# Reordering the first units of a fused state-space scan and two-layer projection on one Trainium2 core

## The chip, the cores and the metric

The kernel runs on one core of a Trainium2 chip. The time is that of the device in microseconds (us); lower is better. The engines are called as the profile calls them: PE (TensorE, with PEld for its weight loads), DVE (VectorE), ACT (ScalarE), POOL (GpSimd) and SP (SyncE, here a queue that issues DMAs).

## The reference

Two blocks follow each other. The first is a gated linear recurrence over the sequence, for 4 batches and 8 heads, 768 steps each, with head width 32 and state width 16. Inputs are x, a decay a for each step, B and C:

```
for chunk c:                     # log_a = log(clip(a, 1e-6, 1)); cum = cumsum of it in the chunk
    M       = (C_c B_c^T) * exp(cum_i - cum_j) * causal
    y_c     = M x_c + (C_c state) * exp(cum_i)
    state   = exp(sum of log_a) * state + sum_j (B_j x_j^T) * exp(cum_end - cum_j)
```

The result y, as 3072 rows of 256, goes through the second block: h = y w_in (256 x 2048), g = h * sigmoid(h), out = g w_out (2048 x 256). The two weight matrices arrive in 64 bits and are cut down to 32 by the kernel itself.

## The kernel before, in words

The sequence is cut into chunks of 64 steps, and 256 steps of one batch form a unit; there are 12 units (u = 0 to 11), three for a batch. Two units form a pair P, whose 512 rows go through the second block at a time. Nothing is scheduled by a compiler: the order of the calls in the source is the order of the instructions in each engine's queue, and a queue runs strictly in that order. Semaphores stand where one engine needs another's result or a buffer.

The recurrence of a unit consists of these steps.

- f_P0 clips a (laid over the partitions, tile pa01 for units 0 and 1, pa2 for unit 2) into pz; it runs on POOL at L337. f_P scans it to running products pfx on DVE (L341). f_C multiplies C with them into cw (L400; for unit 0 on POOL, else on DVE).
- f_Ab (L354 to L358) broadcasts the clipped a from 12 rows (ach) to 128 partitions with a PE matmul by a selection matrix, into one PSUM bank (8 heads of 64 steps). There are two for a unit (k = 0, 1). f_Ek (L360) runs scan_E (L346 to L352) over it on DVE: products of a between all pairs of steps in a chunk, tile E. Units 0 to 1 get it so; later units load the rows by DMA instead (load_ab, f_E1).
- f_B (L370) weights B into BT (DVE). f_TP (L382) transposes B, and for unit 1 and 2 also C, on PE. For the first unit of a batch C is loaded in another layout and transposed on DVE by f_T (L378). f_T2 (L396, ACT) splits C by odd and even heads into ce.
- f_G (L424) is C times B on PE and writes the PSUM tile gy; f_D0 (L408) is BT times x on PE, into other columns of the same tile. f_M (L434, DVE) multiplies G into E, once for each k; f_S (L438, DVE) carries the state over the four chunks; f_SM (L453, ACT) masks the states.
- f_Y (L460) makes y on PE, f_X (L484) copies it out on ACT (tile xf).

The weights come in blocks of 256 columns or rows, n = 0 to 15: load_w loads the raw block (SP's queue), w_size (ACT, L193 and L196) and w_bits (DVE, L201, L203, L204, then one add on POOL, L209, in one or two parts) cut it to 32 bits (tile w). POOL's add is the last step, and PE's projection waits for it.

The pair 0 goes through the second block in plain 32-bit products: f_s1(u, j) (L515) is h for block j and one unit, four matmuls and a Silu on ACT; f_s2(j) (L526) adds block j of the second product. From pair 1 on each 32-bit product is done in three faster parts: w_h, w_l (ACT, with an accumulating DMA on POOL's queue) and w_d (DVE) split the weights, f_xh, f_xl and f_xd split y, and s1_d, s1_h and s2, s2_d (L543 to L604) multiply them. step(s), for s = 0 to 82, runs this for pairs 1 to 5 and puts the recurrence of the next pair in between (PLAN). It fills most of the time: from about 80 us on.

Ahead of step(0) the order is written out by hand, in two parts. L654 to L723 is a list of calls for units 0 and 1, weight blocks 0 to 5 and the loads of units 2 and 3. L782 to L790 is the table `steps`, where each entry (u, j, text) is f_s1(u, j) followed by the steps of the text, and then six texts for f_s2. In a text "2:PTC1" means steps P, T, C and the first half of the scan (f_E1) for unit 2; D is f_G and f_D0, S is f_S, s is f_SM, M is f_M twice, Y is f_Y and f_X, and small h, l, d are the parts of y. A step without a colon is one for the weights: b is w_bits, s w_size, h, l, d the three parts, r the load of a raw block, m f_s2, and p s1_d.

At the start PE has nothing to work on. busy (L289) fills this with matmuls of zeros from tile misc (`idle`), which DVE clears at L283; further fills stand at L659 and L671. SP's queue begins with ach (L237), C of unit 0 (L246), a for units 0 and 1 (L249), x of unit 0 (L250) and three raw weight blocks. ACT's queue issues B of unit 0 and C of unit 1 (L247, L248). POOL's queue issues two small stores of f_A0 (L287) and x of unit 2 (L709).

Of the kernel before, what the change touches and what calls it, by code (L numbers as in the profile page):

```python
# [11 lines left out]
BF16 = mybir.dt.bfloat16  # L12
# [21 lines left out]
def kernel(  # L34
# [22 lines left out]
    nc = tc.nc  # L57

    batch, H, S, D = x.shape
# [30 lines left out]
    def half(name):  # L90
        return ps_h.tile([128, 512], FP32, name=name, tag="h")
# [7 lines left out]
    ab, bn, tbc, xt, PZ = ({} for _ in range(5))  # L99
# [16 lines left out]
    def load_n(u, i, q):  # L116
        b, t0 = at(u)
        if i == 0:
            t = bn[u] = (block("bn0")[:, 0:256].rearrange("p (k h n) -> p k h n", k=2, h=H) if u in (0, 1, 3) else
                         loads.tile([128, 2, H, N], FP32, name="bn"))  # L120
        else:
            t = tbc[u] = block("tbc0")[:, 0:256].rearrange("p (k h n) -> p k h n", k=2, h=H)
        for k in range(2):
            q.dma_start(out=t[:, k], in_=(B, C)[i][b, :, t0 + 128 * k:t0 + 128 * k + 128].rearrange("h p n -> p h n"))
# [18 lines left out]
    def load_x(u, q):  # L143
        b, t0 = at(u)
        xt[u] = loads.tile([128, 2, H, D], FP32, name="xt", bufs=2)
        for k in range(2):
            q.dma_start(out=xt[u][:, k], in_=x[b, :, t0 + 128 * k:t0 + 128 * k + 128].rearrange("h p d -> p h d"))
# [41 lines left out]
    def w_size(n, what="uv"):  # L189
        if n in raw:  # L190
            if "u" in what:
                u = wu[n] = block("wu")
                nc.scalar.activation(two(u), raw[n][:, :, :, 1].bitcast(FP32), AF.Abs)  # L193
            if "v" in what:
                v = wv[n] = block("wv")
                nc.scalar.activation(two(v), raw[n][:, :, :, 0], AF.Copy, scale=2.0 ** -51, bias=2.0)  # L196

    def w_bits(n, parts=1):
        if n in raw:
            u, v, hi = two(wu.pop(n)), two(wv.pop(n)).bitcast(U32), raw[n][:, :, :, 1]  # L200
            nc.vector.tensor_scalar(out=u, in0=u, scalar1=LEAST, scalar2=MOST, op0=ALU.max, op1=ALU.min)  # L201
            u = u.bitcast(U32)
            nc.vector.tensor_scalar(out=u, in0=u, scalar1=3, scalar2=None, op0=ALU.logical_shift_left)  # L203
            nc.vector.scalar_tensor_tensor(out=v, in0=hi, scalar=0x80000000, in1=v,  # L204
                                           op0=ALU.bitwise_and, op1=ALU.bitwise_or)
            w32[n] = block("w32")
            for i in range(parts):
                fs = slice(WF // parts * i, WF // parts * (i + 1))
                nc.gpsimd.tensor_tensor(out=two(w32[n])[:, :, fs].bitcast(U32), in0=u[:, :, fs], in1=v[:, :, fs],  # L209
                                        op=ALU.add)  # L210
        if n == 3:
            load_w(n + RAW, nc.sync)
# [22 lines left out]
    A0, A1 = 96, 96 + NC0  # L235
    ach = block("ach").rearrange("p (h t) -> p h t", t=Q)
# [8 lines left out]

    load_t(0, 1, nc.sync)  # L246
    load_n(0, 0, nc.scalar)  # L247
    load_n(1, 1, nc.scalar)  # L248
    load_a(pa01, 0, 2 * UT)  # L249
    load_x(0, nc.sync)  # L250
    for n in range(3):
        load_w(n, nc.sync)
    load_n(1, 0, nc.sync)
# [31 lines left out]
    def f_A0():  # L285
        for t in (a_in[:, :, 0:1].rearrange("h c t -> c h t"), a_zero[:, :, 0:1]):
            nc.gpsimd.dma_start(out=t, in_=misc[:NC1, 0:H].rearrange("p (h t) -> p h t", t=1))  # L287

    def busy(n, small=0):  # L289
        t = half("zero")  # L290
        for i in range(n):
            nc.tensor.matmul(out=t, lhsT=idle[:, 0:128], rhs=idle, start=True, stop=True)
        for i in range(small):
            nc.tensor.matmul(out=t[:64, :64], lhsT=idle[:, 0:64], rhs=idle[:, 64:128], start=True, stop=True)
# [3 lines left out]
    sel = block("sel").rearrange("p (s c t) -> p s c t", s=4, c=2)  # L298
# [11 lines left out]
        nc.gpsimd.affine_select(out=diag1, in_=diag1, pattern=[[0, 1], [-1, Q]], compare_op=ALU.not_equal,  # L310
                                fill=1.0, base=-64 * c, channel_multiplier=1)
    nc.scalar.activation(misc[:, 2 * UT - 1:], idle[:, 0:1], AF.Silu)
    busy(5)
    f_A()
    hm = const.tile([128, H], FP32, name="hm")
    nc.gpsimd.memset(hm, 1.0)
# [17 lines left out]
    def f_P0(u, engine):  # L334
        src = (pa2[:, 0:UT] if u == 2 else pa01[:, UT * u:UT * u + UT]).rearrange("p (c t) -> p c t", t=Q)
        PZ[u] = (pz, pz1, pz)[u]
        engine.tensor_scalar(out=PZ[u][:, :, 1:], in0=src, scalar1=1.0, scalar2=1e-6, op0=ALU.min, op1=ALU.max)  # L337
# [8 lines left out]
    def scan_E(u, g0, n, t):  # L346
        if g0 == 0:
            E[u] = sc.tile([128, 2, H, Q], FP32, name="E")
        nc.vector.tensor_tensor_scan(out=E[u].rearrange("p k h t -> p (k h t)")[:, Q * g0:Q * (g0 + n)],  # L349
                                     data0=t.rearrange("p g t -> p (g t)"),  # L350
                                     data1=diag[:, 0:n].rearrange("p g t -> p (g t)"),
                                     initial=0.0, op0=ALU.mult, op1=ALU.add)  # L352

    def f_Ab(u, k):  # L354
        ab[u, k] = t = acc("ab").rearrange("p (h t) -> p h t", t=Q)
        nc.tensor.matmul(out=t.rearrange("p h t -> p (h t)"),  # L356
                         lhsT=sel[:A1, 2 * u + k].rearrange("r c m -> r (c m)"),
                         rhs=ach[:A1].rearrange("r h t -> r (h t)"), start=True, stop=True)  # L358

    def f_Ek(u, k):  # L360
        scan_E(u, H * k, H, ab.pop((u, k)))

    def f_E1(u, i, n):
        g = 2 * H // n
# [5 lines left out]
    def f_B(u, ks=slice(0, 2)):  # L370
        if u not in BT:
            BT[u] = sc.tile([128, 2, H, N], FP32, name="BT")
        nc.vector.tensor_tensor(out=BT[u][:, ks], in0=bn[u][:, ks],
                                in1=E[u][:, ks, :, Q - 1:Q].to_broadcast([128, ks.stop - ks.start, H, N]), op=ALU.mult)
# [33 lines left out]
    def f_D0(u, ts=(0, 1, 2, 3)):  # L408
        last = u % UPB == UPB - 1
        bt = BT[u].rearrange("p k h n -> p k (h n)")  # L410
        xc = xt[u].rearrange("p k h d -> p k (h d)")
        d = [new_dp(u)[:, c, 256:384].rearrange("p (k x) -> p k x", k=2) for c in range(2)]
        for t in ts[:3 if last else 4]:
            k, c = divmod(t, 2)
            for g in range(4):
                nc.tensor.matmul(out=d[c][32 * g:32 * g + 32, k],
                                 lhsT=bt[64 * c:64 * c + 64, k, 32 * g:32 * g + 32],
                                 rhs=xc[64 * c:64 * c + 64, k, 64 * g:64 * g + 64], start=True, stop=True,
                                 tile_position=(64 * c, 32 * g), skip_group_check=True)
        BX[u] = d  # L420
        if 3 in ts:
            BT.pop(u)

    def f_G(u):  # L424
        bh, ce, dp = BH.pop(u), CE.pop(u), new_dp(u)
        for k in range(2):
            for c in range(2):
                ts = slice(128 * k + 64 * c, 128 * k + 64 * c + 64)
                for g in range(4):
                    nc.tensor.matmul(out=dp[64 * c:64 * c + 64, g, 128 * k:128 * k + 128],  # L430
                                     lhsT=bh[32 * g:32 * g + 32, ts], rhs=ce[32 * g:32 * g + 32, :, ts],
                                     start=True, stop=True, tile_position=(32 * g, 64 * c), skip_group_check=True)

    def f_M(u, k):  # L434
        m = E[u].rearrange("p k (g e) t -> p k g (e t)", e=2)
        nc.vector.tensor_tensor(out=m[:, k], in0=DP[u][:, :, 128 * k:128 * k + 128], in1=m[:, k], op=ALU.mult)
# [216 lines left out]

    f_P0(0, nc.gpsimd)  # L654
    f_P0(1, nc.gpsimd)
    f_Ab(0, 0)
    f_Ab(0, 1)
    f_TP(0)
    busy(2, 18)  # L659
    f_Ek(0, 0)  # L660
    f_Ek(0, 1)
    f_B(0)
    f_D0(0)
    f_T(0, 1)
    for e in range(2):
        f_T2(0, e)
    w_size(0, "u")
    f_P(0)
    f_C(0, nc.gpsimd)
    f_A0()  # L670
    busy(1, 10)  # L671
    f_G(0)
    f_S(0)
    f_SM(0)
    w_size(0, "v")
    f_M(0, 0)
    f_M(0, 1)
    w_bits(0, 2)
    f_Ab(1, 0)
    w_size(1)  # L680
# [14 lines left out]
    load_n(2, 0, nc.scalar)  # L695
    f_P(1)
    f_C(1)
    f_P0(2, nc.gpsimd)
    w_bits(2, 2)
    f_G(1)  # L700
    f_D0(1)
# [9 lines left out]
    load_w(7, nc.sync)  # L711
    load_w(8, nc.sync)
    w_bits(3, 2)
    f_Y(1)
    f_X(1)
    w_size(4)
# [55 lines left out]
    def todo(text):  # L772

        for step in text.split():
            if ":" in step:
# [3 lines left out]
            n = int(step[1:].split(".")[0])  # L779
            {"b": w_bits, "s": w_size, "h": w_h, "l": w_l, "d": w_d, "m": f_s2, "p": s1_d, "r": load_r}[step[0]](n)  # L780

    steps = ((1, 0, ""), (0, 3, "2:PTC1 s6"), (1, 1, "b5 2:2Ba"), (1, 2, "3:x b6 r11 s7"), (1, 3, "b7 r12 s8"),  # L782
             (0, 4, "2:DSsM r13"), (1, 4, "b8 r14 s9"), (0, 5, "s10"), (1, 5, "2:Y 3:TPC"), (0, 6, "3:12B s11"),
             (1, 6, "b9 r15 s12 h0 l0"), (0, 7, "2:h"), (1, 7, "3:DSsM b10 s13"))
    for u, j, text in steps:
        f_s1(u, j)
        todo(text)
    for text in ("m0 b11 2:l h1 l1 d0 s14", "m1 3:Y b12 2:d 4:L 3:h h2 l2 d1 b13 s15", "m2 3:l 3:d d2 b14 h3 l3",
                 "m3 b15 p0 d3 h4 l4 4:T", "m4 h8 l8 d4 h5 l5 d8", "m5 d5 h9 l9 d9"):
        todo(text)  # L790


# [109 lines left out]
```

## Time and profile before

| | |
|---|---|
| median of 3 runs | 336.53 us (335.56 to 336.82) |
| the profiled execution, its own time | 338.14 us |
| its span | 336.4 us |
| mean granted PE clock | 0.986 |
| PE busy / idle in the span | 322.9 / 13.5 us |
| PE busy from 0 to 8, 8 to 16, 16 to 24 us | 6.69, 6.74, 5.06 us |
| PE busy from 24 to 32, 32 to 40, 40 to 50 us | 7.53, 7.75, 9.51 us |
| PE busy from 70 to 80, 320 to 336.4 us | 9.05, 10.63 us |

A matmul at half clock is as busy as one at full clock but does half the work, so the granted clock has to be read beside the busy time. In the stretch from 24 to 32 us it is 0.63; in the other stretches of 8 to 20 us from the start to 320 us it is 1.00, but for 0.94 from 16 to 24. In the timeline and in the chain of waits the first number is the start and the second the length, both in us; brackets show how long the engine was idle before and what ended that.

### The profile page before, as it was taken

Reading aid. Unit: us, or ns where it says so; the run is one execution under the profiler, and the core shown is the slowest. Engines: PE = TensorE matmul, PEld = TensorE weight load, DVE = VectorE, ACT = ScalarE, POOL = GpSimd, SP = SyncE. Lnnn points to the kernel's source line nnn. Section 1 sums busy time; section 2 is a strip of 40 time slices with the busy share of each in tenths; the row PEclk is TensorE's granted clock in tenths of the full one; section 3 lists DMA queues with packets and bytes.
Section 4 is the critical chain, followed back from the end, with each engine's and each line's share of the span. In section 5 each row is a group of like instructions: output and inputs, shape, how many; then the busy total and the mean of one; then the engine's idle time right before and its main releaser. Section 6 shows DMA issues by size and latency. Waiting matters only on the chain.

```text
span 336.4 us, 7749 instructions
## 1 busy us (share of the span) xinstructions
PE 322.9 (96%) x3138; PEld 256.4 (76%) x3138; DVE 251.9 (75%) x415; ACT 218.1 (65%) x417; POOL 75.7 (23%) x75
## 2 busy tenths in 40 slices
PE   7869999989999999999999999999999999999993
PEld 3547878878878778878788878788778788888882
DVE  6893795998877888997965996875996863574453
ACT  2644857555578898766666666767666756666651
POOL 3544342356211222231202231202240202000000
PEclk9987999999999999999999999999999999999998
DMA  7899678753776584164420164510253000012003
GB/s 116 219 277 291 172 173 268 143 90 63 128 146 105 102 158 88 43 115 72 103 50 0 47 111 83 113 29 0 59 105 60 2 2 0 0 25 40 0 0 62
DMA packets 94699, 30.80 MB, mean 92 GB/s; under 512 B 79612, under 2 KB 85756, under 8 KB 94664
## 3 DMA queue, kind: packets, MB, share of 16 engines
q1 hardware_dynamic: 83848, 25.20, 33.8%
q0 software_dynamic: 2464, 4.46, 7.6%
q10 hardware_dynamic: 8352, 0.66, 1.7%
q8 instruction: 24, 0.39, 0.5%
q14 instruction: 11, 0.09, 0.1%
HBM read 22.79 MB, written 3.32 MB: 78 GB/s over the span
## 4 chain that ended last, share of the span: by engine, by line
PE 79%; DVE 10%; DMA 5%; issue 2%; SPq 1%; ACT 1%; POOL 0%; DVEq 0%; ACTq 0%; POOLq 0%
PE hp L555 23%; PE hp L547 11%; PE b L603 11%; PE oa L589 11%; PE oa L590 11%; PE oa L532 4%; PE gy L479 2%; PE hp L519 2%; DMA tbc<-in_C_dram 2%; PE gy L470 2%; PE gy L430 2%; DVE wv L204 2%; DVE E L349 2%; DMA pa<-in_a_dram 1%; DMA xt<-in_x_dram 1%
## 5 line engine op out<-in xcount | busy, mean ns | idle before, releaser
L549 ACT ACTIVATE hp<-hp 128x512 f32<-128x512 f32 x80 | 46.6, 582 | 69.8 <-PE hp L547 69.8
L569 DVE TENSOR_TENSOR gl<-g,gh 128x512 fp32r<-128x512 f32 x62 | 42.7, 689 | 48.9 <-ACT gh L565 45.7
L555 PE MATMUL hp<-xh,wh 128*128 128x512 f32 x160 | 65.3, 408 | 0.0
L573 DVE SCALAR_TENSOR_TENSOR gd<-gh,g 128x512 fp32r<-128x512 f32 x80 | 59.6, 747 | 5.2 <-ACT gh L565 5.2
L555 PE MATMUL hp<-xl,wl 128*128 128x512 f32 x160 | 62.5, 391 | 0.0
L589 PE MATMUL oa<-gh,wh 128*128 128x512 f32 x160 | 62.4, 390 | 0.0
L590 PE MATMUL oa<-gl,wl 128*128 128x512 f32 x160 | 62.3, 389 | 0.0
L569 POOL TENSOR_TENSOR gl<-g,gh 128x512 fp32r<-128x512 f32 x18 | 29.3, 1630 | 121.8 <-ACT gh L565 121.8
L565 ACT ACTIVATE gh<-g 128x512 fp32r<-128x512 f32 x80 | 50.6, 632 | 2.8
L547 PE MATMUL hp<-xd,wd 128*128 128x512 f32 x160 | 49.4, 390 | 0.9 <-DVE xd L509 0.9
L563 ACT ACTIVATE g<-hp 128x512 f32<-128x512 f32 x80 | 47.5, 594 | 0.5 <-PE hp L555 0.5
L603 PE MATMUL b<-gd,wd 128*128 128x512 f32 x160 | 44.3, 390 | 0.0
L555 PEld LDWEIGHTS hp<-xh,wh 128*128 128x128 f32 x160 | 30.0, 187 | 9.2 <-ACT hp L549 2.6
L547 PEld LDWEIGHTS hp<-xd,wd 128*128 128x128 f32 x160 | 29.9, 188 | 7.8 <-DVE xd L509 1.3
L519 PE MATMUL hp<-xf,w 128*128 128x256 f32 x128 | 31.4, 401 | 4.2 <-POOL w L209 2.9
L603 PEld LDWEIGHTS b<-gd,wd 128*128 128x128 f32 x160 | 30.0, 188 | 6.5 <-DVE o L629 0.3
L589 PEld LDWEIGHTS oa<-gh,wh 128*128 128x128 f32 x160 | 30.0, 188 | 6.4
L590 PEld LDWEIGHTS oa<-gl,wl 128*128 128x128 f32 x160 | 30.0, 188 | 6.3
L555 PEld LDWEIGHTS hp<-xl,wl 128*128 128x128 f32 x160 | 30.1, 188 | 5.2
L519 PEld LDWEIGHTS hp<-xf,w 128*128 128x128 f32 x128 | 24.8, 199 | 9.4 <-POOL w L209 3.9
L209 POOL TENSOR_TENSOR w<-wu,wv 128x512 uint32<-128x512 uint32 (+1 forms) x20 | 24.0, 1207 | 33.4 <-DVE wv L204 33.3
L349 DVE TENSOR_TENSOR_SCAN E<-ab,diag 128x512 f32<-128x512 f32 x24 | 28.4, 1211 | 1.7 <-PE ab L356 1.5
(84 smaller groups left out, 383.9 us busy)
## 6 DMA issues: line engine op xcount, KB each, us to landing
ab<-a_zero SPq DMA_DIRECT2D x18, 256.0 KB
raw<-in_moe_w_in_dram SPq DMA_DIRECT2D x8, 512.0 KB
raw<-in_moe_w_out_dram SPq DMA_DIRECT2D x8, 512.0 KB
wl<-w POOLq DMA_DIRECT2D x16, 256.0 KB, 3.8
xt<-in_x_dram SPq DMA_DIRECT2D x22, 128.0 KB
out_dram<-ot SPq DMA_DIRECT2D x44, 64.0 KB
bn<-in_B_dram SPq DMA_DIRECT2D x20, 64.0 KB
tbc<-in_C_dram SPq DMA_DIRECT2D x20, 64.0 KB
```

Source lines behind the costliest of these rows:

```text
L349: nc.vector.tensor_tensor_scan(out=E[u].rearrange("p k h t -> p (k h t)")[:, Q * g0:Q * (g0 + n)], data0=t.rearrange("p g t -> p (g t)"), ...
L519: nc.tensor.matmul(out=hp[:, i], lhsT=two(w32[j])[:, kc, 128 * i:128 * i + 128], rhs=two(XF[u])[:, kc], start=(kc == 0), stop=(kc == KC - 1))
L547: nc.tensor.matmul(out=HP[s], lhsT=two(WD[f // 2])[:, kc, 128 * (f % 2):128 * (f % 2) + 128], rhs=XD[P][:, kc], start=(kc == 0), stop=Fals ...
L549: nc.scalar.activation(HP[s], HP[s], AF.Copy, scale=-HALF / UP)
L555: nc.tensor.matmul(out=HP[s], lhsT=two(w[f // 2])[:, kc, 128 * (f % 2):128 * (f % 2) + 128], rhs=x_[P][:, kc], start=False, stop=(kc == KC ...
L563: nc.scalar.activation(G[s], HP.pop(s), AF.Silu, scale=UP)
L565: nc.scalar.activation(GH[s], G[s], AF.Copy, scale=DOWN)
L569: engine.tensor_tensor(out=GL[s], in0=G[s], in1=GH[s].bitcast(FP32), op=ALU.subtract)
L573: nc.vector.scalar_tensor_tensor(out=GD[s], in0=GH[s].bitcast(FP32), scalar=1.0 + 1.0 / HALF, in1=G.pop(s), op0=ALU.mult, op1=ALU.subtract)
L589: nc.tensor.matmul(out=OA[P][m], lhsT=two(WH[n])[:, r, ms], rhs=gh, start=(f == 0), stop=False)
L590: nc.tensor.matmul(out=OA[P][m], lhsT=two(WL[n])[:, r, ms], rhs=gl, start=False, stop=(f == NF - 1))
L603: nc.tensor.matmul(out=B2[P][:, m], lhsT=two(WD[n])[:, r, 128 * m:128 * m + 128], rhs=gd, start=(fresh and s == tiles[0]), stop=True, skip ...
```

## The change

It changes the order by hand and three small pieces of the work:

- x of unit 0 is loaded ahead of a. C of unit 1 (load_n(1, 1)) moves from ACT's queue at the very start to POOL's, behind the clips of a for units 0 and 1.
- The first fill, early(6), multiplies a constant tile of ones that POOL writes at the start, and has six matmuls; the fill of 2 + 18 matmuls behind f_TP(0) is gone.
- For unit 0 f_Ab makes each broadcast as two matmuls of 4 heads, and f_Ek scans 4 heads at a time. The transpose and split of C stand between the second and the third of these quarters.
- In unit 0 f_G comes ahead of f_D0, f_M(0, 0) ahead of f_S, and both halves of w_size(0) behind f_M(0, 1) in the source.
- The clip of a for unit 2 (f_P0(2) on POOL) moves from ahead of weight block 2 to behind x of unit 2 and weight block 3.
- In the table and the texts weight blocks go later by a step or so and stand between the steps of units 2 and 3; block 10 comes ahead of S and M of unit 3; s1_d(0) (p0) stands behind f_s2(4) instead of f_s2(3), and the w_d of blocks 0 to 2 and 8 move by one text.

```diff
     load_t(0, 1, nc.sync)
     load_n(0, 0, nc.scalar)
-    load_n(1, 1, nc.scalar)
+    load_x(0, nc.sync)
     load_a(pa01, 0, 2 * UT)
-    load_x(0, nc.sync)
...
+    warm = nc.const_aps.tensor(1.0, [128, 512], BF16)
+
+    def early(n):
+        t = half("zero")
+        for i in range(n):
+            nc.tensor.matmul(out=t, lhsT=warm[:, 0:128], rhs=warm, start=True, stop=True)
...
-    busy(5)
+    early(6)
...
     def f_Ab(u, k):
         ab[u, k] = t = acc("ab").rearrange("p (h t) -> p h t", t=Q)
-        nc.tensor.matmul(out=t.rearrange("p h t -> p (h t)"),
-                         lhsT=sel[:A1, 2 * u + k].rearrange("r c m -> r (c m)"),
-                         rhs=ach[:A1].rearrange("r h t -> r (h t)"), start=True, stop=True)
-
-    def f_Ek(u, k):
-        scan_E(u, H * k, H, ab.pop((u, k)))
+        n = 4 if u == 0 else H
+        for h in range(0, H, n):
+            nc.tensor.matmul(out=t[:, h:h + n].rearrange("p h t -> p (h t)"),
+                             lhsT=sel[:A1, 2 * u + k].rearrange("r c m -> r (c m)"),
+                             rhs=ach[:A1, h:h + n].rearrange("r h t -> r (h t)"), start=True, stop=True,
+                             skip_group_check=True)
+
+    def f_Ek(u, k, hs=slice(0, H)):
+        t = ab[u, k] if hs.stop < H else ab.pop((u, k))
+        scan_E(u, H * k + hs.start, hs.stop - hs.start, t[:, hs])
...
     f_P0(0, nc.gpsimd)
     f_P0(1, nc.gpsimd)
+    load_n(1, 1, nc.gpsimd)
     f_Ab(0, 0)
     f_Ab(0, 1)
     f_TP(0)
-    busy(2, 18)
-    f_Ek(0, 0)
-    f_Ek(0, 1)
-    f_B(0)
-    f_D0(0)
+    f_Ek(0, 0, slice(0, 4))
+    f_Ek(0, 0, slice(4, 8))
     f_T(0, 1)
     for e in range(2):
         f_T2(0, e)
-    w_size(0, "u")
+    f_Ek(0, 1, slice(0, 4))
+    f_Ek(0, 1, slice(4, 8))
+    f_B(0)
+    busy(1, 10)
+    f_G(0)
+    f_D0(0)
     f_P(0)
     f_C(0, nc.gpsimd)
     f_A0()
-    busy(1, 10)
-    f_G(0)
+    f_M(0, 0)
     f_S(0)
     f_SM(0)
-    w_size(0, "v")
-    f_M(0, 0)
     f_M(0, 1)
+    w_size(0)
     w_bits(0, 2)
...
     f_C(1)
-    f_P0(2, nc.gpsimd)
     w_bits(2, 2)
...
     w_bits(3, 2)
+    f_P0(2, nc.gpsimd)
     f_Y(1)
...
-    steps = ((1, 0, ""), (0, 3, "2:PTC1 s6"), (1, 1, "b5 2:2Ba"), (1, 2, "3:x b6 r11 s7"), (1, 3, "b7 r12 s8"),
-             (0, 4, "2:DSsM r13"), (1, 4, "b8 r14 s9"), (0, 5, "s10"), (1, 5, "2:Y 3:TPC"), (0, 6, "3:12B s11"),
-             (1, 6, "b9 r15 s12 h0 l0"), (0, 7, "2:h"), (1, 7, "3:DSsM b10 s13"))
+    steps = ((1, 0, ""), (0, 3, "2:PTC1 s6"), (1, 1, "b5 2:2Ba"), (1, 2, "3:x b6 r11 s7"), (1, 3, ""),
+             (0, 4, "2:DSsM r12"), (1, 4, "b7 r13 s8"), (0, 5, "3:T s9"), (1, 5, "2:Y b8 r14"), (0, 6, "3:1PC s10"),
+             (1, 6, "b9 r15 3:2B s11 h0 l0"), (0, 7, "2:h s12"), (1, 7, "3:D b10 3:SsM"))
...
-    for text in ("m0 b11 2:l h1 l1 d0 s14", "m1 3:Y b12 2:d 4:L 3:h h2 l2 d1 b13 s15", "m2 3:l 3:d d2 b14 h3 l3",
-                 "m3 b15 p0 d3 h4 l4 4:T", "m4 h8 l8 d4 h5 l5 d8", "m5 d5 h9 l9 d9"):
+    for text in ("m0 b11 s13 2:l h1 l1", "m1 3:Y b12 s14 2:d d0 4:L 3:h h2 l2", "m2 b13 s15 3:l d1 h3 l3",
+                 "m3 b14 3:d d2 h4 l4 4:T", "m4 b15 p0 d3 h8 l8 d4 h5 l5", "m5 d8 d5 h9 l9 d9"):
         todo(text)
```

## The prediction, made before the result was known

> **What bounds the kernel now.** I read the page's busy shares first, then the busy time by stretches, then the chain of waits in order of time, then the timeline of the first 16 us. The page says that TensorE is the bound:
>
> ```profile
> PE 322.9 (96%) x3138; PEld 256.4 (76%) x3138; DVE 251.9 (75%) x415; ACT 218.1 (65%) x417; POOL 75.7 (23%) x75
> ```
>
> The span is 336.4, so PE idles 13.5 us. In the stretches from 80 to 320 us it idles 0.1; 5.8 lie in the last 16.4, which the change doesn't touch. The other 7.6 lie before 80 us, and only there can the change act. The chain of waits shows the worst place (columns: start, length, what):
>
> ```profile
> 17.50 4.81 DMA pa<-in_a_dram
> ...
> 22.48 0.09 POOL pz L337
> 22.57 0.39 issue
> 22.95 0.74 POOL w L209
> 23.70 0.04 issue
> 23.74 3.78 PE hp L519 x8
> 27.52 1.06 PE gy L470 x32
> 28.59 1.13 PE gy L479 x62
> ```
>
> POOL's clamp of a for unit 2 (L337) waits for its load until 22.48. Behind it in POOL's queue stands the add that finishes weight block 2 (L209), whose operand DVE had ready at 20.96 + 0.69 = 21.65; PE waits for that block. The stretches of one microsecond show what follows (PE busy first; the granted clock stands after POOL):
>
> ```profile
> 20.00:21.00 1.00, 1.00 (x65) 0.74 (x64) 0.97 (x4) 0.60 (x1) 0.00 (x0) 1.00 1.04 381
> 21.00:22.00 1.00, 0.17 (x24) 0.01 (x1) 0.96 (x4) 0.00 (x0) 0.00 (x0) 1.00 0.75 213
> 22.00:23.00 1.00, 0.00 (x0) 0.00 (x0) 0.93 (x4) 0.13 (x1) 0.44 (x2) 1.00 1.04 336
> 23.00:24.00 1.00, 0.26 (x1) 0.26 (x2) 0.98 (x2) 1.00 (x3) 1.00 (x2) 0.54 1.09 250
> 29.00:30.00 1.00, 0.70 (x48) 0.46 (x32) 0.00 (x0) 0.26 (x1) 0.00 (x0) 0.55 1.11 376
> ```
>
> PE idles 2.57 us, and from 23 to nearly 30 its clock is at half. The timeline of unit 0 shows the start:
>
> ```profile
> 5.43 2.45 DVE L349 TENSOR_TENSOR_SCAN E<-ab,diag 128x512 f32<-128x512 f32 x2 [1.50 <-PE ab L356]
> 8.26 0.64 DVE L378 STREAM_TRANSPOSE ct<-tbc 128x256 f32<-128x256 f32 x1
> 8.31 1.32 POOL L337 TENSOR_SCALAR pz<-pa 128x256 f32<-128x256 f32 x2 [4.36 <-DMA pa<-in_a_dram]
> 8.56 0.63 PE L416 MATMUL gy<-xt,BT 64*32 64x64 f32 x32 [0.60 <-DMA xt<-in_x_dram]
> 9.89 0.70 PE L430 MATMUL gy<-ce,bh 32*64 32x128 f32 x32
> 11.78 1.28 DVE L436 TENSOR_TENSOR E<-gy,E 128x512 f32<-128x512 f32 x2
> ```
>
> DVE waits 1.5 us for the first broadcast, scans 2.45, and only then transposes C, which ACT's two scalings (0.91) and G (L430) need. Loads of a and x land together, at about 8.4.
>
> **What the skill says.** "TensorE: Matmul & The Clock Gate", Part 1 (the HAM clock gate): the PE clock falls to half after an idle window of some 3.4 us and returns after a busy one; the windows run free of the kernel. The trace agrees on half and on two such windows (23.0 to 29.8), but an idle of 2.57 us behind 1.1 us of small matmuls was enough. "GPSIMD Engine Reference", section 8: POOL shares SBUF interfaces with VectorE. The trace agrees: the add of L209 took 2.12 us at 38.59 beside a scan, 1.27 at 54.79. "DMA: Bandwidth & Descriptors", Issuing engines are not separate DMA queues: another queue saves issue time only, not transfer time; no run here separates this yet.
>
> **The change part by part.**
>
> *Fill from constants.* The five fills wait for DVE's memset until 1.26; the constants are written by 0.48 and engines start near 0.94, so 0.3 is won; a sixth costs 2.31/5 = 0.46. The first broadcast (3.37) moves by +0.15 (0 to 0.3).
>
> *Broadcast and scan by quarters.* The two broadcasts take 3.25 us on PE; halves add weight loads that lie beside matmuls, 0. A scan of 512 takes 1.22, one of 260 (L341) 0.69: 2.1 ns an element and 0.14 fixed. A quarter is 0.68, four are 2.72 instead of 2.45. The first half stands about 1.0 after the start: scans 4.6 to 5.3 and 5.6 to 6.3, transpose to 6.9 (its C landed by 3.5, so the scans queued behind don't wait), two scans to 8.25, f_B (0.42) to 8.7. That is 0.35 later for f_B, but the transpose ends 2.0 earlier.
>
> *Loads.* Unit 1's C (128 KB in short rows) leaves the front. From 2 to 5 us the DMA moved 138 + 102 + 155 = 395 KB, 132 GB/s, so this is worth 1.0 us: x lands near 6.8, a near 7.4 (7 to 8.4). On POOL it costs two issues, 1.89 us by the row of x(2), ahead of f_C, f_A0's two issues (1.65) and weight block 0. Clamps 7.4 to 8.7, issues to 10.6, f_C (0.69) to 11.3, f_A0 to 13.0. Y(0) wants f_C's result at 12.0 and block 0 wants POOL at 14.0: hidden by 0.7 and 1.0; without that cover, up to 1.9. It must land before PE's transposes of unit 1 near 16.7; POOL's loads of x(2) took 4.9 to 5.9 from issue to landing, so 15.5 to 16.5: hidden, barely. ACT's queue is freed of 1.27 us of issues; its first work on data is at 6.88, so 0.
>
> *Order of unit 0.* Scalings of C to 7.85; G 8.0 to 8.7; D0 to 9.4; prefix scan (0.69) to 9.4; M(0,0) (0.64) to 10.1; S (1.15) to 11.25; M(0,1) to 11.9 against 13.06. But both halves of w_size(0) now follow SM (0.64): SM to 11.95, two at 0.65 to 13.25, against 12.78. DVE's last op on the block (0.68) ends at 13.95 against 14.46. The first projection (15.47) waits for this block: **0.5 won** (0 to 1.2).
>
> *The clamp of unit 2 moved.* It goes behind block 2, x(2)'s two issues and block 3 on POOL. Its reader (the prefix scan at 32.73) has 5 us to spare. Block 2's add goes from 22.95 to 21.65: **1.3 won** (1.0 to 1.5). PE still idles 2.57 - 1.3 = about 1.3.
>
> *The clock.* Without the dip the row L519 x8 is 1.89 instead of 3.78 (the one at 15.47), L470 0.69 (at 48.80) instead of 1.13 (as the timeline has it): 0.44; L479 0.86 (at 65.94) instead of 1.18: 0.32. Together 1.89 + 0.44 + 0.32 = 2.65. Idles of 0.70 (12.5 us) and 0.94 (74 us) left the clock full, 2.57 did not; 1.3 is nearer the former. As it lies between, and the plain runs are already 1.6 shorter than this execution, I take **2.0** (0 to 2.65).
>
> *Weight blocks among scans.* A block costs DVE 0.42 + 0.43 + 0.68 = 1.53. DVE stands idle 3.98 us until 58.69 for D(3); block 10 now goes into that. ACT's wait of 5.33 for block 10 before xh goes too; PE's second projection (7.17) covered it, so 0. Between S(3) and xd(3) DVE keeps four blocks (11 to 14 instead of 10 to 13), but PE gets one more step of the second projection (7.17/2 = 3.58) ahead of s1_d(0). The wait of 0.94 there goes: **0.9 won**. The loads r12 to r14 go later by one step or so on SP's queue; SP is held there by ab(3) (3.62) anyway, 0.
>
> *What is late next.* PE comes some 3.8 us earlier to D(2), at about 37.9 for the part that needs BT. The rows of a that DVE clamps at L277 land at about 31.8 (SP waits until then). From 32.2 DVE has 0.68 + 0.42 + 1.22 + 1.53 + 1.22 + 0.42 = 5.5, so BT(2) at 37.7 to 38.6: **0.4 lost** (0 to 1). BT(3) was ready at 53.3; it comes 2.8 earlier by BT(2) but has block 9 ahead of it (1.53): 52.0, while PE wants it near 53; one stall beside POOL (0.95) would show: **0.45 lost** (0 to 2).
>
> *Sum.* -0.5 - 1.3 - 2.0 - 0.9 + 0.4 + 0.45 = -3.85. The profiled execution took 338.14 (span 336.4 and 1.7 around it): 334.3. The median of the runs shown is 336.53, 1.6 below that execution, so 332.7 there.
>
> **Rivals.** (B) The clock still falls, since 1.3 us of idle remain. For it: free windows. Against it: the two shorter idles. Then -0.5 - 1.3 - 0.9 and PE isn't ahead of its feeders, 0.5 lost for the clock falling at a busier place: -2.2, 334.3. (C) The bound passes to DVE and its loads from 30 to 58 us: DVE is 9.83 of 10 busy from 40 to 50. For it: the DMA engines are mostly over 0.8 busy from 17 to 35. Against it: DVE idles 4.9, 2.2 and 4.0 us between 26 and 59. With 2.5 more lost at D(2) and D(3): -1.35, 335.2. (D) Slower: unit 1's C from POOL's queue comes too late. PE's transposes stand in order ahead of the second projection of unit 0, and DVE's f_C(1) ahead of block 2. It costs from a landing at 17.2, DVE's slack of 0.8 makes it 18.0; with the clock falling anyway, the 1.3 and 0.9 won are used up at 20.2, and from 21.9 the kernel is slower by 0.5%. Twice the 5.9 us seen, after issues that end at 10.6, would be 22.4: 336.53 + 22.4 - 20.2 = 338.7. For it: DVE's two-input work slows POOL (1.27 to 2.12). Against it: POOL's tiny stores at 10.3 landed within 6.1.
>
> **How the numbers follow.** A 0.58 (332.7, own range 331.2 to 334.4), B 0.14, C 0.14, D 0.14. The bound of 0.5% (1.7 us, about what a measurement of this kernel can tell from no change) lies at 334.85 and 338.2. Faster: A and B less a tail of 0.03, 0.69; within: C and the tail, 0.17; slower: D, 0.14. The range from 331.0 to 335.6 holds A, B and C but for tails of 0.06, and leaves D out.
>
> **What would show it.** Right: block 2's add on POOL starts within 0.2 us of DVE's L204; PE's clock stays full from 20 to 32; the first projection starts near 14.9 and s1_d(0) has no wait on xd; PE's idle before 80 us falls by about 2. Wrong: PE waits at L386 for unit 1's C, a clock under 0.9 in any early stretch, waits of PE for BT at L416 over 1 us, or DVE waiting longer at L277 while PE waits behind it.

## The result and the profile after

The changed kernel takes 334.45 us (median of 20 runs), the kernel before 336.67 beside it (20 runs). The ratio of the two is 0.9939 with an interval of 0.9921 to 0.9957: 2.05 us faster (1.4 to 2.7). The forecast was 3.85 us faster; the time lies inside the range. The experiments below show that the sign was forecast for largely wrong reasons.

The profiled execution of the changed kernel took 334.14 us, with a span of 332.4. The first line of the page's busy times shows the same PE share with 3.9 us less of it. Some 2.65 of these are the half-clock stretch that the profile before had caught; idle time ahead of 80 us fell by 0.3 only (7.7 to 7.4), where the forecast named about 2:

```profile
PE 319.0 (96%) x3123; PEld 254.9 (77%) x3123; DVE 253.8 (76%) x417; ACT 218.2 (66%) x417; POOL 77.6 (23%) x77
```

In the busy times by microsecond (PE first, the clock after POOL) PE is still idle at 22 us, for 1.33 us in all, but its clock stays full:

```profile
21.00:22.00 1.00, 0.95 (x64) 0.61 (x63) 0.97 (x4) 0.58 (x1) 0.00 (x0) 1.00 0.99 211
22.00:23.00 1.00, 0.00 (x0) 0.00 (x0) 0.93 (x4) 0.00 (x0) 0.50 (x1) 1.00 1.17 236
23.00:24.00 1.00, 0.72 (x3) 0.67 (x4) 0.96 (x3) 0.66 (x3) 1.00 (x3) 1.00 0.97 225
```

The timeline of the start answers the lines on unit 0:

```profile
5.46 1.27 DVE L355 TENSOR_TENSOR_SCAN E<-ab,diag 128x256 f32<-128x256 f32 x2 [1.50 <-PE ab L364]
6.65 0.62 DVE L388 STREAM_TRANSPOSE ct<-tbc 128x256 f32<-128x256 f32 x1
8.26 0.70 PE L440 MATMUL gy<-ce,bh 32*64 32x128 f32 x32 [0.96 <-ACT ce L406]
9.60 1.32 POOL L343 TENSOR_SCALAR pz<-pa 128x256 f32<-128x256 f32 x2 [5.61 <-DMA pa<-in_a_dram]
10.97 2.07 POOL L124 DMA_DIRECT2D tbc<-in_C_dram  x2
13.03 0.72 POOL L410 TENSOR_TENSOR cw<-ct,pfx 128x256 f32<-128x256 f32 x1
13.81 0.58 PE L480 MATMUL gy<-cw,sm 32*64 32x64 f32 x24 [2.55 <-POOL cw L410]
```

The transpose of C and G start 1.6 us earlier; 1.9 to 2.0 had been worked out. But the clip of a starts at 9.60 instead of 8.31, and Y(0) (L480) waits 2.55 us for cw, which stands on POOL behind the two issues for unit 1's C. The first projection starts at 16.11, before at 15.47: the new start loses 0.64 us.

The chain of waits in order of time shows the next place:

```profile
4.15 5.36 DMA pa<-in_a_dram
...
22.51 0.72 POOL w L209
23.23 0.04 issue
23.28 1.99 PE hp L529 x8
...
33.62 0.44 DVE cw L410
34.06 0.04 issue
34.10 5.45 PE hp L529 x24
```

L529 x8 takes 1.99 instead of 3.78, at full clock. At 33.6 PE waits for DVE's cw of unit 2, because DVE had waited 2.92 us for the rows of a (L276, at 32.46). A projection of unit 0 waits for it because cw is what reads the PSUM tile tp last, and in the source tp and hp take turns in the same two buffers. Three positions on PE serve as marks for all runs, each from the timeline of its profiled execution in us: the third projection of unit 0 (what the moved clip releases), the first of the second projection (f_s2(0)), and the first s1_h.

| kernel | clock at half, early | third projection | f_s2(0) | s1_h(0) | median | ratio to before (interval) |
|---|---|---|---|---|---|---|
| before | 23.1 to 29.9 | 23.74 | 58.33 | 82.13 | 336.67 | |
| changed | no | 23.28 | 55.36 | 77.94 | 334.45 | 0.9939 (0.9921 to 0.9957) |
| e1_clip_only | no | 22.49 | 56.81 | 80.62 | 336.54 | 0.9991 (0.9974 to 1.0007) |
| e2_fill_only | no | 24.59 | 56.82 | 80.47 | 336.79 | 0.9991 (0.9975 to 1.0007) |
| e3_table_only | no | 24.32 | 55.59 | 78.18 | 334.71 | 0.9926 (0.9897 to 0.9955) |
| e4_start_only | 13.3 to 16.7 | 23.36 | 56.73 | 80.53 | 337.11 | 1.0015 (0.9993 to 1.0036) |
| e5_a_first | 13.8 to 20.6 | 24.06 | 56.68 | 79.27 | 334.22 | 0.9928 (0.9908 to 0.9948) |
| e6_clamp_pool | no | 23.30 | 56.20 | 78.80 | 335.41 | 0.9950 (0.9932 to 0.9969) |
| e7_c_behind | no | 22.99 | 54.90 | 77.50 | 334.62 | 0.9936 (0.9915 to 0.9956) |
| e8_joined | no | 21.57 | 56.15 | 78.73 | 335.38 | 0.9937 (0.9904 to 0.9970) |
| e9_steps_only | no | 23.26 | 54.53 | 77.12 | 334.94 | 0.9965 (0.9934 to 0.9997) |
| e10_texts_only | 23.8 to 30.7 | 24.85 | 59.44 | 82.03 | 335.56 | 0.9975 (0.9954 to 0.9995) |
| e11_feed | 13.7 to 17.1 | 22.98 | 55.27 | 77.87 | 333.99 | 0.9940 (0.9920 to 0.9960) |
| e12_feed_joined | no | 21.53 | 54.21 | 76.80 | 333.04 | 0.9908 (0.9871 to 0.9944) |

Ratios are to runs of the kernel before on the same chip, whose medians were 336.74 (e1 to e4, 60 runs), 336.75 (e5 to e8, 16) and 336.44 us (e9 to e12, 46). They are not the quotients of these medians. As the chips differ, the runs are compared by the ratios. The marks are of one execution each: that of e9, for one, is the fastest of its 14 (333.22).

### The profile page after: what moved, and what is told of

It is laid out like the page before. It is cut to its first block, busy times and chain, and to the rows that moved or that the text cites. A ratio compares the mean times of both kernels' runs of the same rounds, so it can differ in the third digit from the quotient of the medians.

```text
span 332.4 us, 7727 instructions
## 1 busy us (share of the span) xinstructions
PE 319.0 (96%) x3123; PEld 254.9 (77%) x3123; DVE 253.8 (76%) x417; ACT 218.2 (66%) x417; POOL 77.6 (23%) x77
## 4 chain that ended last, share of the span: by engine, by line
PE 90%; DVE 3%; issue 2%; DMA 2%; SPq 1%; ACT 1%; POOL 1%; DVEq 0%; POOLq 0%; ACTq 0%
PE hp L565 23%; PE b L613 11%; PE hp L557 11%; PE oa L599 11%; PE oa L600 11%; PE oa L542 8%; PE hp L529 8%; PE gy L489 3%; PE gy L480 2%; PE gy L440 2%; DMA pa<-in_a_dram 2%; PE gy L426 1%; POOL w L209 1%; SPq L135 0%; DVE wv L204 0%
## 5 line engine op out<-in xcount | busy, mean ns | idle before, releaser
L613 PEld LDWEIGHTS b<-gd,wd 128*128 128x128 f32 x160 | 29.9, 188 | 6.5 <-DVE o L639 0.3
L529 PE MATMUL hp<-xf,w 128*128 128x256 f32 x128 | 29.8, 386 | 3.0 <-POOL w L209 1.7
L355 DVE TENSOR_TENSOR_SCAN E<-ab,diag 128x512 f32<-128x512 f32 (+1 forms) x26 | 29.2, 1153 | 2.0 <-PE ab L364 1.5
L209 POOL TENSOR_TENSOR w<-wu,wv 128x512 uint32<-128x512 uint32 (+1 forms) x20 | 24.1, 1212 | 27.2 <-DVE wv L204 27.1
L529 PEld LDWEIGHTS hp<-xf,w 128*128 128x128 f32 x128 | 23.7, 190 | 8.0 <-POOL w L209 2.8
```

The costliest lines, as they stand in the source:

```text
L529: nc.tensor.matmul(out=hp[:, i], lhsT=two(w32[j])[:, kc, 128 * i:128 * i + 128], rhs=two(XF[u])[:, kc], start=(kc == 0), stop=(kc == KC - 1))
L613: nc.tensor.matmul(out=B2[P][:, m], lhsT=two(WD[n])[:, r, 128 * m:128 * m + 128], rhs=gd, start=(fresh and s == tiles[0]), stop=True, skip ...
```

## The experiments

My theory after the result: the clip and the clock gained most of it, the table some, and the start gave back 0.6. The rival was that the start had gained and the clip nothing; a third reading, that the early parts don't matter at all, came out of the first four runs.

**e1_clip_only.** The kernel before, with the clip of unit 2 moved.

```diff
     f_C(1)
-    f_P0(2, nc.gpsimd)
     w_bits(2, 2)
...
     w_bits(3, 2)
+    f_P0(2, nc.gpsimd)
```

> The kernel before with one edit: the clip of a for unit 2 goes behind weight block 3 on POOL. Theory (the gain of the change comes from here): block 2's add follows DVE's L204 at once, the third projection of unit 0 starts near 22.5 instead of 23.74 us, the clock stays full in most executions; 1.2 to 3.5 us faster than before. Rival (the start is what gained): at most 0.5 us faster.

The local claim held, the time didn't follow: 0.9991. The timelines of PE and DVE show why. The bracket is the engine's idle before the line and what ended it:

```profile
22.49 1.99 PE L519 MATMUL hp<-xf,w 128*128 128x256 f32 x8 [1.33 <-POOL w L209]
26.52 0.75 PE L479 MATMUL gy<-E,xt 64*32 64x64 f32 x52 [1.15 <-issue]
27.74 3.72 PE L519 MATMUL hp<-xf,w 128*128 128x256 f32 x16 [0.47 <-ACT xf L489]
32.02 0.33 PE L386 MATMUL tp<-ident,bn 128*128 128x128 f32 x1 [0.45 <-DMA bn<-in_B_dram]
32.89 0.42 DVE L277 TENSOR_SCALAR acl<-acl 36x512 f32<-36x512 f32 x1 [2.83 <-DMA acl<-in_a_dram]
34.05 0.42 DVE L400 TENSOR_TENSOR cw<-tp,pfx 128x256 f32<-128x256 f32 x1
34.53 5.45 PE L519 MATMUL hp<-xf,w 128*128 128x256 f32 x24 [0.23 <-DVE cw L400]
40.89 3.72 PE L519 MATMUL hp<-xf,w 128*128 128x256 f32 x16
```

**e2_fill_only.** The kernel before, with fills in the idle, so that the clock can't fall and the wait stays.

```diff
     f_D0(1)
+    busy(10)
```

> The kernel before with ten fill matmuls (0.22 us each) behind D0(1), in the idle of PE from 21.2 to 23.7 us; POOL's wait stays. Theory (the idle lets the clock fall, at a cost of 2.65 us): the third projection of unit 0 still starts near 23.7, its row of eight takes 1.9 us, and the time is 1.5 to 2.7 us below before. Rival (the clock falls for another reason, or rarely): within 0.7 us of before.

The rival's side came: 0.9991. The same view of PE, to set beside e1:

```profile
24.59 1.99 PE L519 MATMUL hp<-xf,w 128*128 128x256 f32 x8 [1.28 <-POOL w L209]
28.47 3.72 PE L519 MATMUL hp<-xf,w 128*128 128x256 f32 x16 [0.47 <-ACT xf L489]
32.88 7.17 PE L519 MATMUL hp<-xf,w 128*128 128x256 f32 x32 [0.25 <-ACT gT L522]
40.96 3.72 PE L519 MATMUL hp<-xf,w 128*128 128x256 f32 x16
```

In e1 PE starts the third projection 2.10 us earlier than in e2. It then waits 1.15 in the middle of Y(1), 0.45 for B of unit 2 and 0.23 for cw, and at 40.9 both stand at the same place (40.89 and 40.96). So the moved clip removes a stall of PE, and all of it is paid back within 18 us. (Part of the 2.10 is chance: with the clip in its old place the third projection starts at 23.26 in e9 and at 24.85 in e10.) What sets the limit is the last of these waits. The rows of a land, DVE clamps them at 32.89 in e1 and 32.90 in e2, and cw ends at 34.47 and 34.48; PE can't pass that point sooner, wherever it stood before. For the wait of 1.15 the profile names no releaser. PE stands still in Y(1) in e4, e6, e7, e11 and e12 too (0.18 to 1.14 us), each time behind its 27th matmul there, and why isn't known.

As to the clock: of the 60 runs of the kernel before beside these four, 34 have a mean clock of 0.995 or more, with a median of 336.25; 7 have 0.99 or less, with a median of 338.65, 2.4 us more and near the 2.65 worked out. Beside e9 to e12, on another chip, 10 of 45 have 0.99 or less, and are 1.6 us slower than those at 0.995 or more. The mean is a rough sign only, as it takes in the end of the kernel, where PE has no work: e9's profile has 0.994 with a full clock up to 326 us. In e1 and e2 no run is under 0.994, so both edits did keep the deep falls away, and neither kernel is faster by it. So a deep fall is real and costs some 2 us, it comes in a minority of the executions, and the profile of before had caught one. How many of the runs in between hold a shorter one isn't known.

**e3_table_only.** The kernel before with the new `steps` and texts, and nothing else of the change.

> The kernel before with the new table and texts only. Theory: PE's wait of 0.94 us for xd ahead of s1_d(0) goes, and waits for ACT at 34 and 47 us shrink; 0.7 to 1.5 us faster. Rival (DVE becomes late at D(3), block 9 being ahead of BT): PE waits at D0(3), same time as before or slower.

This is the whole gain: 0.9926, 2.5 us (1.5 to 3.5), which can't be told from the changed kernel. PE even waits longer for block 2 than before, with no fall of the clock, and meets no wait at s1_d(0) (L547):

```profile
24.32 1.99 PE L519 MATMUL hp<-xf,w 128*128 128x256 f32 x8 [3.30 <-POOL w L209]
...
55.59 7.17 PE L532 MATMUL oa<-gT,w 128*128 128x256 f32 x32
63.99 10.63 PE L532 MATMUL oa<-gT,w 128*128 128x256 f32 x48
74.27 0.81 PE L547 MATMUL hp<-xd,wd 128*128 128x512 f32 x2
```

**e4_start_only.** The changed kernel with the old table and the old place of the clip.

> The kernel before with the new start only (loads, fills, quarters, order of unit 0); clip of unit 2 and table as before. Theory (the start loses 0.64 us, as a for unit 0 lands at 9.5 instead of 8.2): first projection near 16.1; the wait of POOL for a of unit 2 to 22.3 swallows it, so the time is within 0.5 us of before, or up to 0.7 slower. Rival (as I forecast): 0.5 us or more faster.

1.0015, 0.5 us slower by the middle of the interval, not clear of zero. The start gained nothing. It also brought a new place for the clock to fall: PE idles 1.84 us ahead of Y(0) for cw, and in the busy times by microsecond the clock is at half from 13.3 on. Of the eight profiles with the new start three show such a fall (e4, e5, e11); that of the changed kernel doesn't.

```profile
13.00:14.00 1.00, 0.87 (x32) 0.76 (x40) 0.97 (x3) 1.00 (x3) 1.00 (x3) 0.63 0.83 104
14.00:15.00 1.00, 1.00 (x64) 0.85 (x64) 0.56 (x1) 0.30 (x1) 0.75 (x2) 0.50 0.88 109
```

**e5_a_first.** The changed kernel with a ahead of x again on SP's queue.

```diff
-    load_x(0, nc.sync)
     load_a(pa01, 0, 2 * UT)
+    load_x(0, nc.sync)
```

> The changed kernel with a for units 0 and 1 again ahead of x of unit 0 on SP's queue. Theory (x ahead holds a back, and a releases the chain to weight block 0): clips of a start near 8.0 instead of 9.6, the first projection near 15.2 instead of 16.1, 0.5 to 1.0 us faster than the changed kernel. Rival (the load of unit 1's C or the raw weights hold it back): clips still after 9, same time.

The first half held: POOL's clips start at 7.87.

```profile
7.87 1.32 POOL L343 TENSOR_SCALAR pz<-pa 128x256 f32<-128x256 f32 x2 [3.95 <-DMA pa<-in_a_dram]
9.26 2.07 POOL L124 DMA_DIRECT2D tbc<-in_C_dram  x2
11.31 0.73 POOL L410 TENSOR_TENSOR cw<-ct,pfx 128x256 f32<-128x256 f32 x1
```

The first projection starts at 15.46, though all of it at half clock (3.75 us instead of 1.99). The second half failed: 0.9928, not told apart from the changed kernel's 0.9939.

**e6_clamp_pool.** The changed kernel with the clamp of the rows of a (L276) on POOL.

```diff
-        nc.vector.tensor_scalar(out=acl[r], ...
+        nc.gpsimd.tensor_scalar(out=acl[r], ...
```

> The changed kernel with the clamp of the rows of a for units 3 on (L276) on POOL instead of DVE. Theory (DVE waits there 2.9 us for the load and PE's second half of unit 0 then waits for cw of unit 2): DVE's prefix scan for unit 2 starts near 31.3 instead of 32.8, PE's wait of 0.54 us for cw goes; 0.4 to 0.8 us faster. Rival (PE is held by other things there): same time.

PE's wait for cw went, but the run is no faster (0.9950). In its profile ACT's issue of B of unit 2 starts at 23.93 instead of 22.21, the masks of unit 1 behind it at 25.04 instead of 23.34, and Y(1) loses 0.50 for the masks and 0.87 in its middle. Why the issue started so late wasn't settled, so this run decides nothing on the clamp.

**e7_c_behind.** The changed kernel with load_n(1, 1) behind f_C(0) on POOL.

```diff
-    load_n(1, 1, nc.gpsimd)
...
     f_C(0, nc.gpsimd)
+    load_n(1, 1, nc.gpsimd)
```

> The changed kernel with the load of unit 1's C behind f_C(0) on POOL's queue. Theory: f_C(0) starts near 11.0 instead of 13.0, Y(0) near 13.0 instead of 13.8; the first projection still waits for weight block 0, so the time changes by less than 0.3 us, unless C lands after 17.7 and PE waits at the transposes of unit 1. Rival (Y(0) sets the start of the first projection): 0.6 to 0.8 us faster.

As the theory had it: Y(0) at 12.87, the first projection at 15.82 waiting 0.53 for weight block 0, and the time the same (0.9936). PE didn't wait for unit 1's C, so the load has room on POOL's queue.

**e8_joined.** The edits of e5, e6 and e7 together, and the first half of w_size(0) ahead of the masks:

```diff
     f_D0(0)
+    w_size(0, "u")
     f_P(0)
...
-    w_size(0)
+    w_size(0, "v")
```

> The changed kernel with a ahead of x, the clamp on POOL, unit 1's C behind f_C(0), and the first half of w_size(0) ahead of SM on ACT again. Theory: the first projection starts near 14.6, 1.5 us earlier than in the changed kernel, and the wait for cw goes; 1.5 to 2.3 us faster than it. Rival (what is won at the start is lost at the weight loads, which land when the DMA engines let them): under 0.7 us faster.

The rival's number held (0.9937, as the changed kernel), its reason only in part: PE waits for a load, but not for a weight block. The first projection starts at 14.40, 1.7 us earlier, the third at 21.57, and f_s2(0) at 56.15, later than in the changed kernel. The chain of waits names the place (start, length):

```profile
22.90 9.67 DMA bn<-in_B_dram
32.58 0.04 issue
32.62 0.55 PE tp L396 x3
33.17 7.17 PE hp L529 x32
```

B of unit 2 is 128 KB in rows of 64 bytes, in two issues from ACT's queue. The second half, issued at 22.9, lands at 32.6. PE idles 2.71 us for it. This load and the rows of a, which DVE or POOL clamps at 31.7 to 33.8 in the runs with the new start that leave both loads in place, are the wall that the early parts run against.

**e9_steps_only** and **e10_texts_only.** The kernel before with one half of the table each: in e9 the new `steps` and the old texts (s13 kept at the end of `steps`), in e10 the old `steps` without s13 and the new texts.

> The kernel before with the new table only (blocks 7 to 10 later, block 10 ahead of S and M of unit 3), the old texts, s13 kept at the table's end. Theory (half of the gain comes from the table: block 7 no longer stands ahead of S(2) on DVE, so ACT's masks and the Silu behind them aren't late): PE's wait of 0.5 to 0.7 us for gT near 45 goes, the second projection starts near 55.6 instead of 56.8; block 10 gone from behind M(3), the wait for xd shrinks too; 1.2 to 2.0 us faster. Rival (the gain comes from p0 standing one step later): under 0.5 us.

> The kernel before with the new texts only (s1_d(0) behind the fifth step of the second projection, blocks spread), the old table without s13. Theory: PE's wait of 0.8 to 0.9 us for xd goes and nothing else; 0.6 to 1.0 us faster. Rival (DVE is then late elsewhere): PE waits for xd or wd at or after the fifth step, same time.

From f_s2(0) to s1_h(0) the kernel before takes 23.80 us (e1 23.81, e2 23.65, e4 23.80). The changed kernel takes 22.58, and e3, e9 and e10 take 22.59 each. So the wait for xd goes by either half alone, and the 1.2 us are had once. From the third projection to f_s2(0), with a full clock throughout, e2 takes 32.23, and e3 and e9 take 31.27: 0.96 more, by `steps` alone. (e10's profile has the clock at half there and isn't compared.) All of it arises between 40 and 47 us, in the three projections ahead of Y(2): from their start to Y(2) the profiles with the old `steps` (before, e1, e2, e4, e10) take 6.13 to 6.40 us, all nine with the new ones 5.37 or 5.38. The times agree with this order, but not sharply: e9 1.2 us faster (0.1 to 2.2, where the marks say 2.2), e10 0.8 (0.2 to 1.5).

The two waits that go, on PE in the profile before:

```profile
46.88 1.99 PE L519 MATMUL hp<-xf,w 128*128 128x256 f32 x8 [0.49 <-ACT gT L522]
74.85 0.73 PE L547 MATMUL hp<-xd,wd 128*128 128x512 f32 x2 [0.94 <-DVE xd L509]
```

The timelines of DVE and ACT tell what `steps` removes between 40 and 48 us. Before (st is S(2), sm the mask, gT a Silu that frees PE's buffer):

```profile
42.47 1.38 POOL L209 TENSOR_TENSOR w<-wu,wv 128x512 uint32<-128x512 uint32 x1 [1.76 <-DVE wv L204]
42.76 1.37 DVE L203 TENSOR_SCALAR wu<-wu 128x512 uint32<-128x512 uint32 x1
44.66 0.90 DVE L450 SCALAR_TENSOR_TENSOR st<-st,pfx,gy 128x64 f32<-128x64 f32 x3
45.65 0.70 ACT L457 ACTIVATE sm<-st,par 128x128 f32<-128x128 f32 x2 [3.26 <-DVE st L450]
46.25 0.57 ACT L522 ACTIVATE gT<-hp 128x512 f32<-128x512 f32 x1
```

and in e3_table_only:

```profile
40.85 0.91 DVE L450 SCALAR_TENSOR_TENSOR st<-st,pfx,gy 128x64 f32<-128x64 f32 x3 [0.34 <-PE gy L416]
41.86 0.69 ACT L457 ACTIVATE sm<-st,par 128x128 f32<-128x128 f32 x2 [1.44 <-DVE st L450]
42.72 0.60 ACT L522 ACTIVATE gT<-hp 128x512 f32<-128x512 f32 x1 [0.17 <-PE hp L519]
```

Block 7 stood on DVE ahead of S(2), which started 1.9 us after PE had ended D(2), in e3 0.1 us after. Nearly half of that comes from one step of block 7 (L203): it takes 1.37 us beside POOL's add of block 6, here and in e1, e2, e4 and e10 alike, and 0.43 where POOL is at rest. S(2) was late, so ACT's mask of unit 2 was late, and the Silu behind it in ACT's queue too; PE waited for that Silu, 0.49 us in the profile before, 0.69 in e2. With block 7 behind S(2) and M(2), PE's wait is gone. That `steps` does it is shown; that it is block 7 and not another of the moves in `steps` is read from the timelines, and no run moves block 7 alone.

**e11_feed.** The changed kernel with B of unit 2 on SP's queue behind C of unit 2, and the rows of a right behind, both ahead of raw block 6.

```diff
     f_A()
+    load_n(2, 0, nc.sync)
+    f_A1()
...
-    load_n(2, 0, nc.scalar)
...
-    f_A1()
```

> The changed kernel with B of unit 2 on SP's queue behind C of unit 2, and the loads of the rows of a for units 3 on right behind it, ahead of raw block 6. Theory (from 28 to 34 us these two small loads, which land near 32 because they share the DMA engines with the raw blocks, hold PE and DVE): the clamp on DVE near 29.3 instead of 32.5, no wait of PE for cw; 0.5 to 1.0 us faster than the changed kernel. Rival (raw block 6, now later, or DVE's own work is next): within 0.3 us of it.

PE's wait for cw is gone (7.17 us without a break from 32.28), and the clamp runs at 30.66, not as early as 29.3. The time is that of the changed kernel (0.9940), so the rival held; f_s2(0) comes 0.1 earlier, although the clock fell at 13.7 in this profile. In e9, where nothing was done to these loads, the clamp ran at 30.66 too, so its place differs that much between executions.

**e12_feed_joined.** e11 with the start of e8, the clamp on DVE.

> As the run before, and a ahead of x, unit 1's C behind f_C(0), the first half of w_size(0) ahead of SM. Theory (a start 1.7 us earlier was lost in the wait of 2.7 us for B of unit 2): first projection near 14.4, no wait for B of unit 2, second projection from about 53.8; 1.2 to 2.0 us faster than the changed kernel. Rival (raw blocks land when the DMA engines let them): PE waits for a weight block between 20 and 45 us, under 0.5 us faster.

The lowest ratio of all: 0.9908 (3.1 us faster than before, 1.9 to 4.3), by the ratios 1.0 us faster than the changed kernel, short of the 1.2 that the theory asked for; by the mark at s1_h(0) 1.14 earlier. The intervals of the two overlap, so that it is the faster one isn't certain. The timeline of PE:

```profile
14.36 1.99 PE L531 MATMUL hp<-xf,w 128*128 128x256 f32 x8 [0.15 <-POOL w L209]
21.53 1.99 PE L531 MATMUL hp<-xf,w 128*128 128x256 f32 x8 [1.33 <-POOL w L209]
30.20 7.62 PE L531 MATMUL hp<-xf,w 128*128 128x256 f32 x32
53.82 0.46 PE L428 MATMUL gy<-xt,BT 64*32 64x64 f32 x32 [0.50 <-DVE BT L385]
```

With the same early start as e8 it starts its next projections at 30.20, e8 at 33.00. Of the 1.75 us won at the first projection, 1.15 are left at f_s2(0); the next wait is for BT of unit 3 (0.50), which the forecast had named as late.

## Why the prediction was right, and where its steps failed

The sign and the range held, the size was nearly twice too large, and the terms were mostly in the wrong places. That the time still fell in the range is luck: 3.8 us forecast for clock, clip and start came to about nothing, and the table brought more than twice its forecast. The range that reading A gave for itself, 331.2 to 334.4, was just missed, and reading B's 334.3 was nearly met, though the clock was not what decided. Profile against profile the two kernels differ by 4.0 us (338.14 and 334.14), close to the 3.85, because the profile before holds the fall of the clock that most executions lack.

- **The clock (2.0 forecast, about 0 measured in the median).** The price was about right: 2.65 worked out, 2.4 and 1.6 between runs with a low and a high mean clock. The failing step was "I take 2.0": the forecast saw that the plain runs were 1.6 us shorter than the profiled execution, and nevertheless took the same fall off their median. e2, which removes the fall alone, is at 0.9991. The rule from idle lengths failed as well: at the same place e3 idles 3.30 us and keeps its clock, e10 3.29 and loses it, and e4 loses it after 1.84.
- **The clip of unit 2 (1.3 forecast).** PE's stall did shrink (3.30 in e3, where it stays; 1.33 in e1), and none of it reached the end: e1 is at 0.9991. What the forecast called rival C happened to this term: the bound went over to the rows of a, to cw behind them and, in part, to B of unit 2, between 26 and 41 us. The forecast gave C 0.14 as a whole and took only 0.4 off for that stretch, at BT of unit 2, which no run showed as a wait. (It set 37.9, where f_G of unit 2 would start, as the time for BT; f_D0, which reads BT, starts 0.62 later in the line of before.)
- **The start (0.5 won forecast, 0.64 lost at the first projection in the profile, e4 at 1.0015).** The step on the loads failed. x's two issues (1.05 us) stand ahead of a, and a landed at 9.5, not 7.4. With a first (e8) it lands at 7.8, issued at 3.05 and not 4.15. And taking unit 1's C out of the front was worth next to nothing, not the 1.0 estimated from bytes moved: with a first, POOL's clips start at 7.69 to 8.31 in the six profiles with C in front (before, e1, e2, e3, e9, e10), and at 7.41 to 7.87 in the three without it (e5, e8, e12), with medians of 7.85 and 7.86. And cw on POOL, "hidden by 0.7", wasn't: f_C ended at 13.75 instead of 11.3. The step that both halves of w_size(0) behind the masks cost 0.5 was not tried alone.
- **The table (0.9 forecast, about 2 by the marks: 0.8 to 1.0 and 1.2).** The wait for xd was priced well (0.94 as a wait, 1.2 in all). Missed was the wait of PE for ACT's Silu. The profile had it, 0.49 us at 46.88, and the forecast priced a weight block only as DVE time. It didn't follow what was queued behind SM(2) on ACT.
- **Late next (0.85 forecast).** Something was late, cw of unit 2 (0.54) and not BT. The forecast's own sum had cw at about 33.3 (32.2 + 0.68 + 0.42), behind the rows of a; it followed DVE's chain on to BT and didn't ask who waits for the PSUM tile that cw reads. BT of unit 3 was late only in e12 (0.50).

On the sum of the four parts: the table alone gives what the whole change gives. Rival B, the clock still falling, did not decide, though the new start gave the clock a new place to fall. D did not happen: unit 1's C took a median of 4.3 us from POOL's queue, and PE didn't wait for it.

## What to carry to other kernels

Before a stall is taken as gain, look for the next load or engine that is waited for at the same place within the next twenty microseconds, and ask when it lands; here an early stall of 2 us was worth nothing and a small reordering of the queues 20 to 50 us later was worth all. A profiled execution that is slower than the median of plain runs may hold an event that most runs don't have, and a term for that event must not be taken off their median. Behind a late instruction, price what is queued on its engine, not the instruction.

## What the runs showed of the hardware

- The Trainium skill, "TensorE: Matmul & The Clock Gate", Part 1, has the clock windows run free of the kernel. The traces fit: half-clock stretches of 3.4 us (e4, e11) and of 6.8 us (before, e5, e10), after idles of 1.5 to 3.3 us, and the same idle at the same place with the fall (e10, 3.29) and without it (e3, 3.30).
- The second half of a load of 128 KB in 64-byte rows took 9.67 us from issue to landing from ACT's queue, beside raw blocks of 512 KB on SP's queue (e8). From SP's queue, behind C of unit 2, the same load no longer held PE (e12), though its two issues there lasted 6.14 us. "DMA: Bandwidth & Descriptors", Queues, rings and completion order, says that each DMA engine takes turns between queues, packet by packet; a packet of small rows would then wait for a packet of a raw block at each turn. That fits, but no run here counts the turns, and e12 also starts the issue 0.5 us earlier than e8 and puts raw block 6 behind it.
- One issue of a raw block on SP's queue, at 20 to 23 us, lasted 3.61 us (before, 22.40) to 7.08 us (e1, 20.25), and everything behind it waited, the rows of a among them. The next issue of a raw block, at 27.2 us, took 0.39 us (changed kernel).
- A step of DVE that takes 0.43 us alone (L203) took 1.37 us beside POOL's add L209 (before, 42.76), and the add took 2.12 us beside a scan of DVE (before, 38.59) and 1.27 us alone (54.79).
